# Float64 weights narrowed by a scaled upper word, and the mix as eight tiles side by side

## The chip, the core and the metric

The kernel runs on one core of a Trainium2 chip. A core has TensorE (PE, matrix products into PSUM), VectorE (DVE), ScalarE (ACT), GpSimd (POOL, which does not reach PSUM in this kernel) and SyncE (SP, whose queue issues every DMA of this kernel). Each engine has a queue of its own, filled in the order in which the program is written; semaphores hold an instruction until what it reads is written and what it overwrites is free. The metric is the device time of one execution in microseconds, as the median of several runs.

## What is computed

The inputs are q, k, v (8 batches, 8 heads, 576 rows, 64 columns), phi (the same with 32 columns), and three weight arrays. The reference, cut to what matters:

```python
a = exp(phi - phi.max(axis=2)); a /= a.sum(axis=2) + 1e-9       # softmax over the 576 rows
k_m, v_m = einsum('bhsm,bhsd->bhmd', a, k), einsum('bhsm,bhsd->bhmd', a, v)
s = q @ k_m.T / sqrt(64);  p = softmax(s, axis=-1)                # over the 32 memory slots
x = (p @ v_m) as (batch, 576, 8*64)
gate = sigmoid(sum over k<5 of conv_w[k] * x shifted down by 4-k rows)
out = (gate * (x @ w_val)) @ w_out
```

The weights w_val, conv_w and w_out come to the chip as float64 and are narrowed there to float32. Each float64 is two 32-bit words, and only integer and float32 operations are used on them.

## The kernel before

All 8 heads of a batch are handled in G = 2 groups of HG = 4 heads; four heads of 32 slots fill 128 partitions. The 576 rows are cut into two halves s of HALF = 288 columns, and the 512 channels into NP = 4 tiles t of two heads each (PG = 2 tiles for a group). The program is a set of small step functions, and the string ORDER lists every call (step, batch, group, half, tile); the engines' queues get their instructions in just that order. Where a step may run on two engines, `pick` takes the first unless the call ends in a star. So phi_sub.0.0* runs on DVE, and soft_mul.0.0 without a star on POOL.

One batch b goes as follows. The step phi_max, phi_turn, phi_top, phi_spread, phi_lay, phi_sub and phi_exp make the exponentials of phi. For each group, slots (L404) multiplies them with k, v and a column of ones; slots_inv and slots_scale divide; slots_turn (L434) transposes, slots_place copies the result; scores (L450) multiplies by q into two PSUM banks `cv`; scores_turn (L459, DVE) transposes to `st`. Then comes the softmax over the slots, for both groups in one instruction each (for batch 0 a group at a time): soft_max, soft_sub (L481), soft_exp (ACT), soft_sum, soft_inv, soft_mul (L505), and soft_turn (L510), which transposes back to `pT`. soft_high and soft_low split pT in a rounded part pH (ACT) and a rest pL (POOL). val_rows (L534) multiplies the memory values with w_val; val_high and val_low split the result into vwH and vwL; val_again appends a copy of the first 64 columns behind the last ones, so that a pair of heads can also be read rotated by one head.

The gate needs a causal convolution with 5 taps, and it is made in two ways. conv (L578) does it on PE: the taps are multiplied into the memory values (step taps, L563), and 5 x 8 products of 32 slots by 64 columns are accumulated. Its product for head j and half s goes to tile and partition half t, x = divmod((j - s) % 4, 2): in the second half the heads are rotated by one, so that the eight products (4 heads, 2 halves) lie in eight different places of the array (row group j, column half x). sigmoid (L622) follows on ACT. The second way is for group 1 of the batches in VECTOR_CONV (1 to 6): mix (L598) multiplies pT by the memory values alone, eight products of 292 columns, with t, x = divmod(j, 2) in both halves, so that the two halves of one head lie in the same place of the array. Then tap (L605) does the convolution: tap 0 on ACT (L608), taps 1 to 4 on DVE (L612), each as one instruction over both halves (128 partitions, 2 x 288 columns), with the tap's weight per partition from cwP; open_gate (L617) is the sigmoid.

The rotation of the second half is carried on: `swapped(b, g)` tells for which groups it holds, value (L633) then reads vwH and vwL 64 columns further, and project (L663) uses a second copy of w_out with its rows rotated (woH[1], woL[1]; step wo_pair, six DMAs within SBUF per pair of tiles). value is 6 products of 288 columns into a PSUM bank `b`, gated multiplies it with the gate (L642, DVE), gated_high and gated_low split it (ACT, POOL), project is 12 products, place copies to SBUF, store writes out.

The PSUM rings are the two-bank tile `cv` with 2 buffers (used by warm, scores, conv and mix) and the bank `b` with 4 (all other products). The loads wait for a free buffer in the ring `raw` (4 buffers), and the narrowing writes to the rings hH and hL (4 each).

Narrowing one weight tile (conv_w is tile c.0, of 8 x 320; w_val v.0 to v.3 and w_out o.0 to o.3, 128 x 512 each) is six instructions: narrow_bits (DVE, L269) shifts the upper word left by 3 and masks it; narrow_sign (DVE, L276) puts the upper bits back in; narrow_round (ACT, L284) scales the lower word down to a rounding count; narrow_add (POOL, L290) adds it; narrow_size (ACT, L294) squares the upper word as a float; narrow_done (DVE, L301) compares it with a threshold and multiplies. From cw_sb (the narrowed conv_w) spread_taps (L307) and turn_taps (L317) lay the taps out by PE. The step warm(n) multiplies the identity by itself n times on PE and keeps nothing; fp32 products show as two records each in the trace.

## Time and profile before

| what | us |
|---|---|
| median of 3 runs (275.67 to 277.62) | 275.68 |
| the profiled execution, its own time | 277.1 |
| its span, first to last instruction | 275.3 |
| PE busy in it | 263.3 |
| DVE busy in it | 197.2 |
| ACT busy in it | 157.9 |
| POOL busy in it | 128.1 |

The span is the time on the profile's own scale; the execution's own time lies 1.8 us above it, and 1.4 us above the median of the runs without a profile. A busy PE is not PE at its peak, since the ends of matmuls are modelled; how densely it works is read from the starts of its matmuls and from the chain of work that ended last.

### The profile page before, as it was taken

The page shows a single profiled execution, that of the slowest core. Times are in us where ns is not written, and L with a number is a line of the kernel's source. Part 1 is how long each engine was busy: PE and PEld are TensorE (multiplying, and loading weights), DVE is VectorE, ACT ScalarE, POOL GpSimd, SP SyncE. Part 2 cuts the span into 40 slices and gives each one's busy share as a digit, 9 for nine tenths or more (in the row PEclk, how much of TensorE's full clock was granted, in tenths as well). Part 3 has the DMA queues.
Part 4 walks back from the last instruction along what each step waited for, and adds up shares of the span by engine and source line. Part 5 has one row for each costly group of instructions (what it writes and reads, how often), then busy time and mean ns, then how long its engine had stood idle before and what let it go on. Part 6 is the DMA issues. An engine that isn't in the chain of part 4 may idle for free.

```text
span 275.3 us, 7706 instructions
## 1 busy us (share of the span) xinstructions
PE 263.3 (96%) x3312; PEld 227.5 (83%) x3312; DVE 197.2 (72%) x294; ACT 157.9 (57%) x265; POOL 128.1 (47%) x112
## 2 busy tenths in 40 slices
PE   7999779999899999999999999999999999999995
PEld 7879567777987988888968988898869888888995
DVE  3889999897847886697939785899589756931300
ACT  3544659766656465475666556836648655472511
POOL 4461759973425372383148152925247814252410
PEclk9979979999999999999999999999999999999999
DMA  6999972499985475065815393347632120121012
GB/s 198 369 359 416 344 254 62 146 251 258 401 318 181 172 243 207 14 255 174 297 53 192 121 355 122 114 201 236 240 127 90 45 88 2 44 88 43 2 68 107
DMA packets 13234, 49.95 MB, mean 181 GB/s; under 512 B 1672, under 2 KB 2184, under 8 KB 10256
## 3 DMA queue, kind: packets, MB, share of 16 engines
q1 hardware_dynamic: 13200, 49.46, 51.5%
q8 instruction: 26, 0.43, 0.7%
q14 instruction: 8, 0.07, 0.1%
HBM read 37.92 MB, written 9.44 MB: 172 GB/s over the span
## 4 chain that ended last, share of the span: by engine, by line
PE 79%; DVE 11%; ACT 3%; DMA 3%; issue 2%; SPq 2%; POOL 0%; POOLq 0%
PE b L663 31%; PE b L633 19%; PE cv L578 8%; PE b L404 6%; PE cv L221 5%; PE cv L450 3%; DMA woH<-woH 3%; DVE st L481 2%; PE b L534 2%; PE cv L598 2%; PE b L434 2%; DVE st L459 2%; DVE st L505 2%; DVE mm L474 2%; DVE pT L510 1%
## 5 line engine op out<-in xcount | busy, mean ns | idle before, releaser
L214 POOL TENSOR_TENSOR hL<-h,hH 128x576 fp32r<-128x576 f32 x32 | 47.6, 1495 | 76.6 <-ACT hH L211 68.8
L663 PE MATMUL b<-hL,woH 128*128 128x288 f32 x256 | 76.9, 300 | 1.9 <-DVE vwL L214 1.0
L663 PE MATMUL b<-hH,woL 128*128 128x288 f32 x256 | 75.5, 295 | 0.0
L663 PE MATMUL b<-hH,woH 128*128 128x288 f32 x256 | 75.4, 294 | 0.0
L663 PEld LDWEIGHTS b<-hL,woH 128*128 128x128 f32 x256 | 48.0, 187 | 8.4 <-issue 3.0
L642 DVE TENSOR_TENSOR h<-b,gate 128x288 f32<-128x288 f32 x64 | 27.9, 452 | 35.5 <-PE b L633 27.8
L663 PEld LDWEIGHTS b<-hH,woH 128*128 128x128 f32 x256 | 48.2, 188 | 0.0
L663 PEld LDWEIGHTS b<-hH,woL 128*128 128x128 f32 x256 | 48.1, 188 | 0.0
L211 ACT COPY o<-b 128x288 f32<-128x288 f32 x56 | 21.4, 399 | 36.7 <-PE b L663 30.8
L612 DVE SCALAR_TENSOR_TENSOR gate<-cv,cwP,gate 128x576 f32<-128x576 f32 x48 | 37.6, 814 | 4.7 <-ACT gate L608 3.9
L211 ACT CAST hH<-h 128x576 fp32r<-128x576 f32 x32 | 21.3, 673 | 22.9 <-DVE h L642 22.2
L214 POOL TENSOR_TENSOR pL<-pT,pH 128x1152 fp32r<-128x1152 f32 (+1 forms) x9 | 21.6, 2406 | 27.0 <-ACT pH L211 27.0
L633 PE MATMUL b<-pL,vwH 128*128 128x288 f32 x128 | 29.4, 311 | 0.0
L578 PE MATMUL cv<-pT,taps 32*64 32x288 f32 x800 | 27.0, 406 | 0.6 <-DVE pT L510 0.6
L633 PE MATMUL b<-pH,vwL 128*128 128x288 f32 x128 | 27.3, 294 | 0.0
L633 PE MATMUL b<-pH,vwH 128*128 128x288 f32 x128 | 27.3, 294 | 0.0
L221 PE MATMUL cv<-ident 128*128 128x128 f32 x152 | 23.0, 316 | 2.0 <-POOL ident masks.py:199 2.0
L633 PEld LDWEIGHTS b<-pL,vwH 128*128 128x128 f32 x128 | 20.1, 188 | 5.4 <-issue 2.4
L221 PEld LDWEIGHTS cv<-ident 128*128 128x128 f32 x152 | 21.7, 228 | 2.6 <-POOL ident masks.py:199 2.0
L578 PEld LDWEIGHTS cv<-pT,taps 32*64 32x64 f32 x800 | 17.4, 131 | 7.5 <-issue 2.8
L404 PE MATMUL b<-kv,e 128*32 128x129 f32 x640 | 21.5, 286 | 0.7 <-ACT e L395 0.7
L290 POOL TENSOR_TENSOR hH<-hH,hL 128x512 int32<-128x512 int32 (+1 forms) x9 | 13.1, 1461 | 17.3 <-DVE hH L276 7.2
(75 smaller groups left out, 428.5 us busy)
## 6 DMA issues: line engine op xcount, KB each, us to landing
kv<-in_kv_dram SPq DMA_DIRECT2D x16, 1032.0 KB, 8.2
out_dram<-o SPq DMA_DIRECT2D x30, 288.0 KB, 3.0
q<-in_q_dram SPq DMA_DIRECT2D x7, 1152.0 KB, 5.1
e<-in_phi_dram SPq DMA_DIRECT2D x7, 640.0 KB, 7.2
kv<-in_kv_dram SPq DMA_DIRECT2D x16, 129.0 KB, 9.1
raw<-in_w_val_dram SPq DMA_DIRECT2D x4, 512.0 KB, 6.8
raw<-in_w_out_dram SPq DMA_DIRECT2D x4, 512.0 KB, 9.2
q<-in_q_dram SPq DMA_DIRECT2D x2, 576.0 KB, 9.0
```

The lines of the kernel that those rows point to most:

```text
L211: eng.copy(out=out, in_=x) if eng is nc.scalar else eng.tensor_copy(out=out, in_=x)
L214: eng.tensor_tensor(out=out, in0=x, in1=hi.bitcast(F32), op=ALU.subtract)
L221: nc.tensor.matmul(ps[:, i % 2, 0:P], lhsT=ident, rhs=ident, start=True, stop=True)
L290: nc.gpsimd.tensor_tensor(out=a, in0=a, in1=r, op=ALU.add)
L404: nc.tensor.matmul(km[j * M:(j + 1) * M, 0:2 * D + 1], lhsT=e[:, g, j * M:(j + 1) * M, c], rhs=x[:, c, j, :], start=(c == 0), stop=(c == C ...
L434: nc.tensor.transpose(out=ps[:, x], in_=live["kvd", b, g][:, x], identity=ident)
L450: nc.tensor.matmul(sc[j * M:(j + 1) * M, s, 0:HALF], lhsT=live["kvT", b, g][rows, 0, j * M:(j + 1) * M], rhs=live["q", b][rows, g, j, :], ...
L578: nc.tensor.matmul(cv[t][x * D:(x + 1) * D, s, 0:HALF], lhsT=w[rows, i, :], rhs=p[rows, g, s * HALF + i:(s + 1) * HALF + i], start=(i == 0 ...
L612: nc.vector.scalar_tensor_tensor(out=gt, in0=x, scalar=w, in1=gt, op0=ALU.mult, op1=ALU.add)
L633: nc.tensor.matmul(vp[:, 0:HALF], lhsT=a[:, t // PG, n:n + P], rhs=p[:, g, s * HALF:(s + 1) * HALF], start=(i == 0), stop=(i == len(parts) ...
L642: nc.vector.tensor_tensor(out=live["h", b, s, y][:, i], in0=live["vp", b, s, t][:, 0:HALF], in1=live["gate", b, t][:, s], op=ALU.mult)
L663: nc.tensor.matmul(ps[:, 0:HALF], lhsT=w[:, t, n * P:(n + 1) * P], rhs=a[:, t % 2], start=(i == 0), stop=(i == len(parts) - 1))
```

## The change

The change has two parts and a new ORDER. First, narrowing: ACT now scales the upper word, read as a float, by 2^-112 (narrow_size, which comes first and writes the tile), DVE shifts that left by 3 and clears the sign (narrow_bits, now from the tile), POOL adds as before, and DVE's narrow_done takes the sign from the raw word with one AND and one OR. narrow_sign is gone; an ACT instruction now stands ahead of the first DVE one, and the raw tile is read to the end. Second, mix uses the same rotation as conv, so that its eight products lie in eight places. With that all groups of all batches are rotated: swapped is gone, val_again copies both groups in every batch, and the two halves of a mix tile hold different heads, so tap is one instruction for each half with a weight column of its own (cwP has twice the columns, and turn_taps makes them by 40 products of one column instead of 10 of two).

```diff
+    def narrow_size(w, t):
+        raw = live["raw", w, t]
+        live["na", w, t] = narrow_tile("hH", raw)
+        nc.scalar.activation(out=live["na", w, t], in_=raw[:, :, 1].bitcast(F32), func=AF.Copy, scale=2.0 ** -112)
...
     def narrow_bits(w, t):
-        raw = live["raw", w, t]
-        a = live["na", w, t] = narrow_tile("hH", raw)
-        nc.vector.tensor_scalar(out=a.bitcast(I32), in0=raw[:, :, 1], scalar1=3, scalar2=0x3FFFFFF8,
-                                op0=ALU.logical_shift_left, op1=ALU.bitwise_and)
-    @step
-    def narrow_sign(w, t):
         a = live["na", w, t].bitcast(I32)
-        nc.vector.scalar_tensor_tensor(out=a, in0=live["raw", w, t][:, :, 1], scalar=-0x40000000, in1=a,
-                                       op0=ALU.bitwise_and, op1=ALU.bitwise_or)
+        nc.vector.tensor_scalar(out=a, in0=a, scalar1=3, scalar2=0x7FFFFFFF, op0=ALU.logical_shift_left,
+                                op1=ALU.bitwise_and)
...
-    def narrow_size(w, t):
-        nc.scalar.activation(out=live["nr", w, t], in_=live["raw", w, t][:, :, 1].bitcast(F32), func=AF.Square)
...
     def narrow_done(w, t):
-        nc.vector.scalar_tensor_tensor(out=o, in0=r, scalar=TINY_HI ** 2, in1=a, op0=ALU.is_ge, op1=ALU.mult)
+        nc.vector.scalar_tensor_tensor(out=o.bitcast(I32), in0=live["raw", w, t][:, :, 1], scalar=-0x80000000,
+                                       in1=a.bitcast(I32), op0=ALU.bitwise_and, op1=ALU.bitwise_or)
...
     def turn_taps(_):
-        for x in range(2):
-            for i in range(KT):
-                nc.tensor.matmul(ps[x * D:(x + 1) * D, i], lhsT=cw_sb[:, 0, i * D:(i + 1) * D],
-                                 rhs=ident[0:H, H - HG + x:H:2], start=True, stop=True)
+        for j in range(HG):
+            for s in range(2):
+                t, x = divmod((j - s) % HG, 2)
+                for i in range(KT):
+                    nc.tensor.matmul(ps[x * D:(x + 1) * D, i, s, t:t + 1], lhsT=cw_sb[:, 0, i * D:(i + 1) * D],
+                                     rhs=ident[0:H, H - HG + j:H - HG + j + 1], start=True, stop=True)
...
     def val_again(b, g, n):
-        gs = slice(0, G if swapped(b, G - 1) else G - 1)
+        gs = slice(0, G)
...
     def mix(b):
-                t, x = divmod(j, 2)
+                t, x = divmod((j - s) % HG, 2)
...
     def tap(b, t, i):
+        for s in range(2):
+            x, w = live["cv", b, t][:, s, i:i + HALF], cwP[:, i, s, t - (NP - PG):t - (NP - PG) + 1]
+            if i == 0:
+                nc.scalar.activation(out=gt[:, s], in_=x, func=AF.Identity, scale=w)
+            else:
+                nc.vector.scalar_tensor_tensor(out=gt[:, s], in0=x, scalar=w, in1=gt[:, s], op0=ALU.mult,
+                                               op1=ALU.add)
...
     def value(b, s, t):
-            n = t % PG * P + (s * D if swapped(b, t // PG) else 0)
+            n = t % PG * P + s * D
...
     def project(b, s, n):
-        parts = [(w[s if swapped(b, t // PG) else 0], live[a, b, s, t // 2], t) for t in range(NP)
+        parts = [(w[s], live[a, b, s, t // 2], t) for t in range(NP)
```

ORDER is written anew as a whole; of its lines one shows the manner (before, then now): `scores.0.1 soft_high.0.0 val_rows.0 scores_turn.0.1 wo_high.0 soft_low.0.0 soft_max.0.1 load_w.o.3 conv.0.0` and `slots_scale.0.1* taps.0.1 slots_turn.0.1 load_kv.1.0 slots_place.0.1 phi_max.1 wo_high.1 scores.0.1 soft_mul.0.0`. Three places matter for what follows.

PE's queue from its start, before (L221 is warm, L361 and L377 turn and spread the maxima of phi, L307 and L317 are the taps, L404 is slots):

```order
L221 MATMUL cv<-ident 128x128 x7
L361 MATMUL b<-ident,mx 128x128
L221 MATMUL cv<-ident 128x128 x5
L377 MATMUL b<-ident,top 128x128
L221 MATMUL cv<-ident 128x128 x12
L307 MATMUL b<-cw_sb,pick_head 128x320 x2
L317 MATMUL b<-ident,cw_sb 64x2 x10
L221 MATMUL cv<-ident 128x128 x7
L404 MATMUL b<-kv_76,e 32x129 x20
```

and now (the same steps stand in lines 214, 352, 368, 296, 308 and 395):

```order
L214 MATMUL cv<-ident 128x128 x8
L352 MATMUL b<-ident,mx 128x128
L368 MATMUL b<-ident,top 128x128
L214 MATMUL cv<-ident 128x128 x8
L296 MATMUL b<-cw_sb,pick_head 128x320
L308 MATMUL b<-ident,cw_sb 64x1 x40
L296 MATMUL b<-cw_sb,pick_head 128x320
L214 MATMUL cv<-ident 128x128 x4
L395 MATMUL b<-kv_76,e 32x129 x20
```

The warming products between turning and spreading the maxima are gone, turn_taps has 40 products where it had 10, and one of the two spread_taps now follows it.

PE's queue ahead of the first value (L633 before, L626 now), before:

```order
L450 MATMUL cv<-q,kvT 32x288 x8
L534 MATMUL b<-w_val_sb,kvT 32x512 x8
L578 MATMUL cv<-pT_72,taps 64x288 x40
L361 MATMUL b<-ident,mx 128x128 x2
L377 MATMUL b<-ident,top 128x128 x2
L221 MATMUL cv<-ident 128x128 x11
L578 MATMUL cv<-pT_72,taps 64x288 x40
L404 MATMUL b<-kv_76,e 32x129 x20
L633 MATMUL b<-pL,vwH 128x288 x2
```

and now (L425 is slots_turn, L441 scores, L525 val_rows, L569 conv):

```order
L368 MATMUL b<-ident,top 128x128 x2
L214 MATMUL cv<-ident 128x128 x6
L569 MATMUL cv<-pT_72,taps 64x288 x40
L395 MATMUL b<-kv_76,e 32x129 x20
L395 MATMUL b<-kv_78,e 32x129 x20
L425 MATMUL b<-ident,kvd 128x128 x4
L441 MATMUL cv<-q,kvT 32x288 x8
L525 MATMUL b<-w_val_sb,kvT 32x512 x8
L569 MATMUL cv<-pT_72,taps 64x288 x40
L626 MATMUL b<-pL,vwH 128x288 x2
```

Now the second conv of batch 0 stands behind batch 1's slots of both groups, its transposes, its first scores and its val_rows, and the first value stands right behind that conv; before, the first value stood behind one slots of batch 1 alone.

DVE's queue at its start, before (the numbers tell the tiles apart; hH is the tile being narrowed, raw the loaded words, L350 is phi_max, L390 phi_sub):

```order
L269 TENSOR_SCALAR hH_112<-raw_102 8x320
L276 SCALAR_TENSOR_TENSOR hH_112<-raw_102,hH_112 8x320
L368 TENSOR_REDUCE top_125<-b_114 128x1
L269 TENSOR_SCALAR hH_130<-raw_104 128x512
L390 TENSOR_TENSOR e_100<-e_100,b_132 128x640
L269 TENSOR_SCALAR hH_153<-raw_108 128x512
L276 SCALAR_TENSOR_TENSOR hH_153<-raw_108,hH_153 128x512
L301 SCALAR_TENSOR_TENSOR cw_sb_81<-hL_110,hH_112 8x320
L269 TENSOR_SCALAR hH_159<-raw_123 128x512
L276 SCALAR_TENSOR_TENSOR hH_159<-raw_123,hH_159 128x512
L276 SCALAR_TENSOR_TENSOR hH_130<-raw_104,hH_130 128x512
```

and now (L268 is narrow_bits, L289 narrow_done, L359 phi_top, L381 phi_sub):

```order
L268 TENSOR_SCALAR hH_111<-hH_111 8x320
L359 TENSOR_REDUCE top_120<-b_118 128x1
L381 TENSOR_TENSOR e_103<-e_103,b_125 128x640
L268 TENSOR_SCALAR hH_123<-hH_123 128x512
L289 SCALAR_TENSOR_TENSOR cw_sb_81<-raw_101,hH_111 8x320
L268 TENSOR_SCALAR hH_146<-hH_146 128x512
L289 SCALAR_TENSOR_TENSOR w_val_sb_80<-raw_105,hH_123 128x512
L268 TENSOR_SCALAR hH_197<-hH_197 128x512
L289 SCALAR_TENSOR_TENSOR w_val_sb_80<-raw_109,hH_146 128x512
L289 SCALAR_TENSOR_TENSOR w_val_sb_80<-raw_115,hH_197 128x512
```

Each tile has two DVE instructions where it had three, and narrow_bits reads the tile that ACT has written instead of the raw words. Elsewhere in the order the first soft_mul of batch 0 (soft_mul.0.0) has moved from DVE to POOL; load_w.o.0 and load_w.o.1 are issued ahead of load_kv.0.1 instead of behind it; the 8 place calls that DVE did go to ACT; and every batch's softmax and mix stand at new distances.

## Rows read from the trace of the kernel before

**Rows 1.** The page of the profile: the span, and the busy time of each engine (share of the span, instructions).
```profile
span 275.3 us, 7706 instructions
...
PE 263.3 (96%) x3312; PEld 227.5 (83%) x3312; DVE 197.2 (72%) x294; ACT 157.9 (57%) x265; POOL 128.1 (47%) x112
```

**Rows 2.** Busy time in us of PE, PE's weight loads, VectorE, ScalarE and GpSimd in stretches of 10 us (in brackets the instructions), then PE's granted clock, the share of DMA time and GB/s.
```profile
10.00:20.00 10.00, 9.63 (x102) 7.96 (x100) 9.39 (x11) 4.72 (x11) 7.23 (x5) 0.83 1.03 357
20.00:30.00 10.00, 9.28 (x140) 7.65 (x140) 9.01 (x17) 5.69 (x11) 2.71 (x3) 1.00 1.02 406
30.00:40.00 10.00, 7.43 (x120) 6.07 (x105) 9.79 (x12) 6.53 (x11) 7.28 (x6) 0.87 0.93 311
...
60.00:70.00 10.00, 8.43 (x129) 6.98 (x128) 7.98 (x14) 6.97 (x12) 3.93 (x6) 1.00 1.03 287
```

**Rows 3.** The chain of work that ended last, in order of time: start, length in us, engine, tile, line, and how many records.
```profile
5.60 1.72 PE cv L221 x10
...
7.43 2.68 PE cv L221 x24
10.12 1.27 PE b L307 x4
11.38 1.04 PE b L317 x20
...
14.63 2.31 PE b L404 x40
16.95 2.47 PE cv L221 x20
...
45.83 2.58 PE b L633 x18
48.41 1.26 PE b L404 x40
...
50.66 0.22 PE b L434 x2
...
51.66 0.65 PE cv L450 x16
...
61.95 7.43 DMA woH<-woH
...
77.77 2.62 PE cv L578 x80
...
86.93 1.02 PE b L534 x16
...
97.69 1.15 PE cv L598 x16
...
259.39 12.81 PE b L663 x96
272.22 0.40 ACT o L211
```

**Rows 4.** Groups of instructions by line and shape: how many, busy us and mean ns of one, the engine's idle time before them and what ended it.
```profile
L612 DVE SCALAR_TENSOR_TENSOR gate<-cv,cwP,gate 128x576 f32<-128x576 f32 x48 | 37.6, 814 | 4.7 <-ACT gate L608 3.9
...
L642 DVE TENSOR_TENSOR h<-b,gate 128x288 f32<-128x288 f32 x64 | 27.9, 452 | 35.5 <-PE b L633 27.8 <-ACT gate L622 5.2 <-ACT gate L617 1.3
...
L390 POOL TENSOR_TENSOR e<-e,mxa 128x1280 f32<-128x1280 f32 x7 | 17.2, 2457 | 3.0 <-ACT mxa L211 3.0
...
L214 DVE TENSOR_TENSOR vwL<-b,vwH 128x512 fp32r<-128x512 f32 x16 | 10.5, 676 | 1.5 <-ACT vwH L211 1.5
...
L276 DVE SCALAR_TENSOR_TENSOR hH<-raw,hH 128x512 int32<-128x512 int32 x8 | 7.5, 947 | 0.2
L598 PE MATMUL cv<-pT,taps 32*64 32x292 f32 x96 | 7.3, 417 | 0.0
```

**Rows 5.** VectorE's instructions in order of time in the first 42 us: start, length, line, operation, shapes.
```profile
7.47 0.82 DVE L390 TENSOR_TENSOR e<-e,b 128x640 f32<-128x640 f32 x1 [0.83 <-PE b L377]
...
21.27 0.78 DVE L459 STREAM_TRANSPOSE st<-cv 128x576 f32<-128x576 f32 x1
...
22.91 0.76 DVE L481 TENSOR_TENSOR st<-st,mm 128x576 f32<-128x576 f32 x1
...
25.54 0.70 DVE L276 SCALAR_TENSOR_TENSOR hH<-raw,hH 128x512 int32<-128x512 int32 x1
...
26.90 1.39 DVE L505 TENSOR_TENSOR st<-st,ss 128x576 f32<-128x576 f32 x1
...
29.03 0.65 DVE L301 SCALAR_TENSOR_TENSOR hH<-hL,hH 128x512 f32<-128x512 f32 x1
...
31.42 1.74 DVE L481 TENSOR_TENSOR st<-st,mm 128x576 f32<-128x576 f32 x1
...
37.49 2.85 DVE L505 TENSOR_TENSOR st<-st,ss 128x576 f32<-128x576 f32 x1
40.37 0.78 DVE L510 STREAM_TRANSPOSE pT<-st 128x576 f32<-128x576 f32 x1
```

**Rows 6.** The same view around the taps of batch 2: eight instructions in a row.
```profile
99.65 6.40 DVE L612 SCALAR_TENSOR_TENSOR gate<-cv,cwP,gate 128x576 f32<-128x576 f32 x8 [0.65 <-ACT gate L608]
```

**Rows 7.** The same view, from the transposes of batch 3's scores to the transpose that ends its softmax.
```profile
115.15 1.45 DVE L459 STREAM_TRANSPOSE st<-cv 128x576 f32<-128x576 f32 x2 [0.26 <-PE cv L450]
...
125.85 1.38 DVE L510 STREAM_TRANSPOSE pT<-st 128x1152 f32<-128x1152 f32 x1
```

More of the change, by code (lines that the diff above doesn't have):

```diff
@@ L1 @@
 import math
-import struct
 from contextlib import ExitStack
@@ new lines @@
+load_phi.1 soft_sum.0.0 slots.0.1 warm.4 wo_high.0 soft_inv.0.0 wo_low.0 load_w.o.2 slots_inv.0.1 narrow_done.o.1
+slots_scale.0.1* taps.0.1 slots_turn.0.1 load_kv.1.0 slots_place.0.1 phi_max.1 wo_high.1 scores.0.1 soft_mul.0.0
+val_rows.0 narrow_size.o.2 scores_turn.0.1 phi_turn.1 warm.3 wo_low.1 val_high.0.1 phi_top.1 soft_max.0.1 val_high.0.0
+phi_spread.1 warm.6 load_kv.1.1 val_again.0.1.vwH phi_lay.1 narrow_bits.o.2 val_again.0.0.vwH narrow_round.o.2
+phi_sub.1 soft_turn.0.0 val_low.0.0 conv.0.0 soft_high.0.0 soft_sub.0.1* val_low.0.1 soft_exp.0.1 load_q.1
@@ new lines @@
+value.1.1.0 gated_low.1.0.0 load_q.3 scores_turn.2.1 phi_exp.3 value.1.1.1 soft_max.2 gated_low.1.1.1 project.1.0.0
+soft_sub.2* keep_v.2 project.1.0.2 load_phi.4 place.1.0.0 gated.1.1.0 soft_exp.2 gated.1.1.1 project.1.0.1 place.1.0.2
+soft_sum.2 gated_high.1.1.0 gated_low.1.1.0 slots.3.0 place.1.0.1 soft_inv.2 store.1.0.0 val_rows.2 load_kv.4.0
+slots_inv.3.0 soft_mul.2* slots_scale.3.0* project.1.1.3 val_high.2.0 taps.3.0 val_high.2.1 soft_turn.2
+val_again.2.0.vwH val_again.2.1.vwH project.1.1.2 val_low.2.0 soft_high.2 mix.2 val_low.2.1 val_again.2.0.vwL
@@ new lines @@
+phi_exp.4 val_again.3.0.vwL project.2.1.2 soft_inv.3 place.2.0.0 place.2.0.3 soft_mul.3* store.2.0.1 slots.4.1
+place.2.1.2 soft_turn.3 slots.4.0 slots_inv.4.1 soft_high.3 mix.3 load_kv.5.0 phi_max.5 project.2.0.1 tap.3.2.0
+soft_low.3 slots_inv.4.0 slots_scale.4.1* tap.3.2.1 slots_scale.4.0* phi_turn.5 project.2.1.0 place.2.0.1 tap.3.2.2
+tap.3.3.0 load_kv.5.1 taps.4.0 tap.3.2.3 value.3.0.2 place.2.1.0 tap.3.2.4 project.2.1.3 phi_top.5 open_gate.3.2
+tap.3.3.1 slots_turn.4.1 project.2.1.1 store.2.0.0 tap.3.3.2 place.2.1.3 gated.3.0.2 slots_place.4.1 store.2.1.1
@@ new lines @@
+tap.3.3.3 slots_turn.4.0 place.2.1.1 value.3.0.3 slots_place.4.0 store.2.1.0 tap.3.3.4 scores.4.0 val_rows.4
+open_gate.3.3 scores_turn.4.0 phi_spread.5 gated.3.0.3 val_high.4.0 conv.3.0 phi_lay.5 val_low.4.0 val_again.4.0.vwH
+val_high.4.1 phi_sub.5 gated_high.3.0.1 val_low.4.1 value.3.1.2 sigmoid.3.0 value.3.1.3 sigmoid.3.1 gated.3.1.2
+gated_low.3.0.1 phi_exp.5 scores.4.1 gated.3.1.3 value.3.0.0 scores_turn.4.1 load_q.5 val_again.4.1.vwH
+val_again.4.1.vwL value.3.0.1 val_again.4.0.vwL soft_max.4 keep_v.4 value.3.1.0 gated_high.3.1.1 gated.3.0.0 slots.5.1
@@ L185 @@
     cwB = const.tile([P, G, KT * D], F32, name="cwB")
-    cwP = const.tile([P, KT, PG], F32, name="cwP")
+    cwP = const.tile([P, KT, 2, PG], F32, name="cwP")
     pick_head = const.tile([H, H, M], F32, name="pick_head")
@@ L195 @@
     steps = {}
-    def swapped(b, g):
-        return g != G - 1 or b not in VECTOR_CONV
     def step(fn):
```

206 lines of the change are left out of this document (89 added, 117 removed).

## Prediction

> **What bounds the kernel now.** I read the page first: PE is busy 96% of the span, DVE 72%, the others less [rows 1]. An average hides stages, so next the busy times in stretches of 10 us: from 10 to 40 us DVE is busy 9.0 to 9.8 of 10 [rows 2]. PE is also busy there, but mostly with warming products, which nobody needs. The chain of work that ended last gives the border: the first value starts at 45.83 us, and from there the chain is almost all PE until its last record ends at 259.39 + 12.81 = 272.20; 3.1 us for the last copy and store close the span at 275.3 [rows 1, 3]. So the kernel has two stages: a start of 45.8 us set by the chain through DVE, and 272.2 - 45.8 = 226.4 us set by PE. PE's only sizeable idle time in the second is in 60 to 70 us, where it is busy 8.4 of 10 and waits for the copies of w_out within SBUF [rows 2, 3]. Each edit is therefore judged by its stage.
>
> **The mix.** It is 1.15 us for 16 records, the same kind of product as conv, which has 2.62 us for 80 [rows 3]. A fifth of conv is 0.524 us; with 292 columns for 288, 0.53. The difference is in the places: conv uses eight, mix four, twice. The mix takes conv's places, so I price it by conv: 1.15 - 0.53 = 0.62 us less, six times, 3.7 us, all in the stage that PE sets. The bounds are nothing and 3.7.
>
> A rule of the Trainium skill speaks against it. TensorEngine Tiling (Array Packing), section Restrictions and Gotchas, states that different row tiles cannot access the same PSUM bank simultaneously. In both kernels two row groups write each bank (tile t, half s), so by that rule the eight products would still take two turns, and the sum would lose its 3.7 us. conv's row speaks for the other side, since its products share banks in the same manner.
>
> **The taps on DVE.** 48 instructions of 814 ns become 96 of half the size [rows 4]. No row shows that form at 288 columns. A half costs at least 407 ns, if nothing in the 814 is fixed, and at most 814. The nearest row is the gating product, also 288 columns from PSUM, at 452 ns [rows 4]. I take 0.45 us: 96 x 0.45 - 48 x 0.81 = 4.3 us more on DVE in all, 0.7 us a batch. It hides as long as conv of the same batch need not wait: conv needs both cv tiles, which the last tap frees. In the new order PE has between mix.1 and conv.1.0 four projects, three values and small transposes, 9.2 us (4 x 1.6, 3 x 0.8, 0.4, at the eight projects in the last 12.8 us of rows 3 and three values in 2.58), 10.0 and 10.4 in batches 2 and 3. Sixteen halves are 7.2 us, and the two first taps on ACT about 1: 8.2, hidden by a margin of 1.0. Before, eight took 6.40 [rows 6].
>
> **Other work that grows or shrinks beside PE.** val_again copies both groups (POOL is busy 47%), eight place copies go from DVE to ACT (57%); both hide in these engines' idle time [rows 1], and I cost them at nothing. If a late copy on POOL held a value, it would be under 1 us each. Narrowing sheds nine narrow_sign (eight of 947 ns [rows 4] and a small one, 8 us of DVE); the later narrow_done has the same form as narrow_sign. All of that lies in the first stage.
>
> **The start.** turn_taps grows from 20 to 80 records. At the 1.04 us that 20 took, 80 take 4.2 us, 3.1 more [rows 3]. What hides it are warming products that go: between the two transposes of the maxima stood 1.72 us of them, and 24 records of 2.68 follow [rows 3], where now there are 16 in all. By these rows the first slots start at 14.7 against 14.63. PE's granted clock is 0.83 in 10 to 20 us and 0.87 in 30 to 40 [rows 2]; eighty tiny products may hold it down, which the 2.31 us of the first slots already contain, against 1.26 for the same work later [rows 3].
>
> From there I compare DVE's lists between two points: the transposing of the first scores (21.27, [rows 5]) and the one that frees the second conv. Before, that one is soft_turn.0.1, ending at 40.37 + 0.78 = 41.15: 19.9 us, nearly dense. Now it is the transposing of scores.1.0, one instruction behind soft_turn.0.1, since scores.1.0 holds a cv buffer that this conv needs. The list in between loses two narrow_sign (1.4) and one soft_mul (1.39, now on POOL), has four narrow_done at 0.70 for one of 0.65 (+2.15), and gains two val_low (1.35), one transpose (0.78) and four short instructions of the division (0.6) [rows 4, 5]: +2.1 us, 22.0 in all. The first point comes about 1 us earlier, at 20.3, because seven warming products instead of ten stand between slots and scores (ten took 2.47, [rows 3]). So the second conv starts at 42.3 + 0.2 and the first value behind it at 42.5 + 2.6 = 45.1.
>
> Two things move that. Two-input operations last longer beside POOL: 1.74 against 0.76 for the same soft_sub, 2.85 against 1.39 for soft_mul [rows 5]. Without such overlap the new list is some 2.3 us shorter, and the first value at 42.8. On the other side, the new order hangs batch 1's slots, division, transposes and scores in front of that conv, a chain through ACT, PE and DVE that waits for POOL's subtraction of 2.46 us [rows 4], and POOL now also has soft_mul.0.0. w_out's first two tiles are loaded ahead of the second group's k and v, whose DMA must wait at SP until narrow_done has released raw tiles: 1 MB at 406 GB/s is 2.6 us [rows 2], landing just ahead of its use. I put 0.7 us on it and take **45.8 us, the same as before**; the bounds are 42.8 and 49.
>
> **The sum.** At its first value PE has by then done more than before: one slots (1.26), two slots_turn (0.44), one scores (0.65), one val_rows (1.02), 3.4 us that no longer stand behind it [rows 3]. So PE's second stage is 226.4 - 3.4 - 3.7 = 219.3 us. The wait for w_out's copies ended about 2 us late before; now the softmax of batch 1 should be late by about as much at mix.1, so no term. The softmax of batch 3 takes from 115.15 to 127.23, 12.1 us [rows 7], while the new order has only 10.8 us of PE work between its scores and its mix (12.4 before): 1.0 us. Together 45.8 + 219.3 + 1.0 + 3.1 = 269.2 against the span of 275.3: 6.1 us less. The profiled execution's own time is 277.1, 1.4 above the median of 275.68; I take the difference off the median: **269.6 us**.
>
> **The rivals.**
>
> *The mix gains nothing.* By a mechanism that serves products of one bank in turn, mix stays at 1.15 us: 269.6 + 3.7 = 273.3 us. Against it: conv at 33 ns a record beside mix at 72 (2.62 over 80, 1.15 over 16, [rows 3]). Chance 0.04. That is the Trainium skill's rule on banks (TensorEngine Tiling, section Restrictions and Gotchas) as a result; by the conv row, the trace disagrees.
>
> *The start eats it.* If batch 1's chain in front of the second conv brings the first value only at 51 us or later, the gain is gone: 269.6 + 5.2 = 274.8 us. For it: DVE is dense there, and one late POOL or DMA step moves everything behind. Against it: 51 needs 5 us beyond a list of DVE that is only 2.1 us longer. Chance 0.14.
>
> *The split taps set the pace; slower.* If a half costs 0.7 us instead of 0.45, taps last 16 x 0.7 + 1 = 12.2 us, and conv waits 3.0, 2.2 and 1.8 us in batches 1 to 3, and some 2 in 5 and 6 each; the values that wait for gates hold their banks besides, so some 10 us: 279.6. The point from which it decides: above 0.51 us a half the margin of batch 1 is gone, and at about 0.65 the whole gain. For it: 814 ns is the upper bound; against it: 452 ns for the nearest shape [rows 4]. Chance 0.08.
>
> **How the numbers follow.** My forecast, with smaller starts and stalls around it, has 0.74. The first value at 42.8 and no stall gives 265.6; at 48.8 with 3 us of stalls 274.6; the first two rivals lie inside. **Range 265.6 to 274.6.** About 1% is what a measurement of this kernel can tell from no change, 2.8 us. Faster by more than that needs under 272.9: 0.74. Within 1%: the late start, the mix without gain, 0.17. Slower: 0.09, the taps and a little for what I don't see.
>
> **What would show it.** Mix at 0.53 us for 16 records, or 1.15. First value near 45.8 us. Taps: mean near 450 ns, and no wait of conv for cv in the batches' middle. From the first value to PE's last record some 220 us. No stall over 1.5 us at mix.3. The prediction fails if the first value is past 50 us, if PE waits at each conv, or if PE's idle time grows at the mixes because the softmax now stands too close to them.

## The result, and the profile after

The changed kernel takes 278.64 us (median of 20 runs, 276.48 to 282.26) against 276.94 for the kernel before (20 runs beside them): ratio 1.0058, 95% interval 1.0036 to 1.0081. The forecast was 269.6, in a range from 265.6 to 274.6. The profiled execution of after is one of its quickest, 276.93 us with a span of 275.2; its granted clock was 0.994 on average, in most of the other runs 0.974 to 0.988, so its profile does not show all of the loss. Ratios compare the runs of a kernel that lie near its fastest; of less_warm below, three of seven runs, the profiled one among them, took 278.0 to 279.2 us at a granted clock of 0.969, the other four 271.7 to 272.7 at 0.987.

The page of after, which answers to [rows 1]: span, and busy time of each engine.

```profile
span 275.2 us, 7826 instructions
...
PE 260.8 (95%) x3338; PEld 224.4 (82%) x3338; DVE 187.1 (68%) x324; ACT 158.1 (57%) x275; POOL 130.9 (48%) x121
```

VectorE has 10 us less to do, and the span is the same. The chain of work that ended last, kernel after: start, length in us, engine, tile, line, records. It answers to [rows 3]; L359 is phi_top, L296 spread_taps, L308 turn_taps, L214 warm, L395 slots, L569 conv, L626 value, L604 the taps on DVE, L589 mix, L656 project.

```profile
6.07 0.30 DVE top L359
...
9.01 0.73 PE b L296 x2
9.74 3.93 PE b L308 x80
...
14.40 2.00 PE cv L214 x8
16.41 1.94 PE b L395 x40
...
38.34 1.77 PE b L395 x54
40.11 0.57 issue
...
44.80 2.23 PE cv L569 x64
47.03 3.02 issue
50.04 0.74 PE cv L569 x16
...
64.42 6.70 DMA e<-in_phi_dram
...
72.55 6.13 DVE gate L604 x15
...
98.52 0.68 PE cv L589 x16
...
259.29 12.81 PE b L656 x96
```

The first value starts at 50.04 + 0.74 = 50.8 us (45.83 before), and PE's last record ends at 272.1 as it did before. So PE's second stage is 221.3 us for 226.4, 5.1 less, and the start has taken back 5.0. Two pieces of it stand in the chain: turn_taps and the warming products behind it, which bring the first slots to 16.41 (14.63 before); and a stop of 3.02 us inside the second conv, behind "issue", where PE waits for nothing that the profile shows (one of 0.57 us stands in the slots before). Further on, the taps of batch 1 begin only at 72.55, since phi_max.3 stands ahead of them on DVE and waits for its load.

Groups by line and shape, after, which answer to [rows 4]: count, busy us and mean ns, idle time before.

```profile
L604 DVE SCALAR_TENSOR_TENSOR gate<-cv,cwP,gate 128x288 f32<-128x288 f32 x96 | 41.7, 508 | 2.1 <-ACT gate L602 2.0
L589 PE MATMUL cv<-pT,taps 32*64 32x292 f32 x96 | 4.5, 430 | 0.0
L308 PE MATMUL b<-ident,cw_sb 8*64 8x1 f32 x80 | 4.0, 193 | 0.0
```

Half a tap takes 508 ns, not 450. The mix's 16 records take 0.68 us (chain), not 0.53 and not 1.15.

### The profile page after: what moved, and what is told of

Read it like the earlier page. It is cut to its first block, busy times and chain, and to the rows that moved or that the text cites. A ratio compares the mean times of both kernels' runs of the same rounds, so it can differ in the third digit from the quotient of the medians.

```text
span 275.2 us, 7826 instructions
## 1 busy us (share of the span) xinstructions
PE 260.8 (95%) x3338; PEld 224.4 (82%) x3338; DVE 187.1 (68%) x324; ACT 158.1 (57%) x275; POOL 130.9 (48%) x121
## 4 chain that ended last, share of the span: by engine, by line
PE 76%; DVE 14%; issue 3%; ACT 3%; DMA 2%; POOL 0%; ACTq 0%; POOLq 0%; DVEq 0%
PE b L656 30%; PE b L626 17%; PE cv L569 9%; PE b L395 6%; PE cv L441 3%; DVE st L472 3%; PE cv L214 3%; DMA e<-in_phi_dram 2%; DVE gate L604 2%; PE b L525 2%; PE b L308 1%; PE b L425 1%; DVE ss L483 1%; DVE mm L465 1%; PE cv L589 1%
## 5 line engine op out<-in xcount | busy, mean ns | idle before, releaser
L207 POOL TENSOR_TENSOR hL<-h,hH 128x576 fp32r<-128x576 f32 x32 | 48.4, 1521 | 66.0 <-ACT hH L204 56.4
L656 PE MATMUL b<-hL,woH 128*128 128x288 f32 x256 | 77.5, 303 | 1.1 <-DVE h L635 0.6
L656 PE MATMUL b<-hH,woL 128*128 128x288 f32 x256 | 75.5, 295 | 0.0
L656 PE MATMUL b<-hH,woH 128*128 128x288 f32 x256 | 75.3, 294 | 0.0
L635 DVE TENSOR_TENSOR h<-b,gate 128x288 f32<-128x288 f32 x64 | 27.3, 450 | 43.0 <-PE b L626 32.6
L656 PEld LDWEIGHTS b<-hL,woH 128*128 128x128 f32 x256 | 48.0, 187 | 8.5 <-issue 4.1
L204 ACT COPY o<-b 128x288 f32<-128x288 f32 x64 | 25.0, 399 | 40.5 <-PE b L656 33.5
L656 PEld LDWEIGHTS b<-hH,woH 128*128 128x128 f32 x256 | 48.2, 188 | 0.0
L656 PEld LDWEIGHTS b<-hH,woL 128*128 128x128 f32 x256 | 48.1, 188 | 0.0
L604 DVE SCALAR_TENSOR_TENSOR gate<-cv,cwP,gate 128x288 f32<-128x288 f32 x96 | 41.7, 508 | 2.1 <-ACT gate L602 2.0
L569 PE MATMUL cv<-pT,taps 32*64 32x288 f32 x800 | 27.9, 406 | 3.6 <-issue 3.0
L204 ACT CAST hH<-h 128x576 fp32r<-128x576 f32 x32 | 21.4, 673 | 14.9 <-DVE h L635 14.2
L626 PE MATMUL b<-pL,vwH 128*128 128x288 f32 x128 | 29.4, 311 | 0.0
L626 PE MATMUL b<-pH,vwL 128*128 128x288 f32 x128 | 27.3, 294 | 0.0
L626 PE MATMUL b<-pH,vwH 128*128 128x288 f32 x128 | 27.3, 294 | 0.0
L569 PEld LDWEIGHTS cv<-pT,taps 32*64 32x64 f32 x800 | 17.5, 131 | 11.3 <-issue 5.1
L626 PEld LDWEIGHTS b<-pL,vwH 128*128 128x128 f32 x128 | 20.1, 188 | 6.0 <-issue 3.8
L395 PE MATMUL b<-kv,e 128*32 128x129 f32 x640 | 21.5, 283 | 1.9 <-ACT e L386 1.4
L395 PEld LDWEIGHTS b<-kv,e 128*32 128x32 f32 x640 | 18.2, 139 | 5.1 <-issue 2.3
L381 POOL TENSOR_TENSOR e<-e,mxa 128x1280 f32<-128x1280 f32 x7 | 18.3, 2618 | 6.1 <-ACT mxa L204 6.0
L626 PEld LDWEIGHTS b<-pH,vwL 128*128 128x128 f32 x128 | 20.5, 188 | 0.0
```

The lines of the kernel that those rows point to most:

```text
L204: eng.copy(out=out, in_=x) if eng is nc.scalar else eng.tensor_copy(out=out, in_=x)
L207: eng.tensor_tensor(out=out, in0=x, in1=hi.bitcast(F32), op=ALU.subtract)
L381: eng.tensor_tensor(out=t, in0=t, in1=mxa.unsqueeze(3).to_broadcast(list(t.shape)), op=ALU.subtract)
L395: nc.tensor.matmul(km[j * M:(j + 1) * M, 0:2 * D + 1], lhsT=e[:, g, j * M:(j + 1) * M, c], rhs=x[:, c, j, :], start=(c == 0), stop=(c == C ...
L569: nc.tensor.matmul(cv[t][x * D:(x + 1) * D, s, 0:HALF], lhsT=w[rows, i, :], rhs=p[rows, g, s * HALF + i:(s + 1) * HALF + i], start=(i == 0 ...
L604: nc.vector.scalar_tensor_tensor(out=gt[:, s], in0=x, scalar=w, in1=gt[:, s], op0=ALU.mult, op1=ALU.add)
```

## The experiments

Fifteen more kernels were measured, each beside the kernel before. The table has for each the ratio to before, and from the chain of its profiled execution the start of the first value, the end of PE's last record and the stage between them. The kernels whose second stage is that of before show 226.4 to 227.1 for it, those with that of after 220.5 to 221.4, which tells how far two profiles of the same agree: differences under 0.9 us are not told apart.

| kernel | ratio (95%) | records of turn_taps | first value | last record ends | second stage |
|---|---|---|---|---|---|
| before | 1 | 20 | 45.8 | 272.2 | 226.4 |
| after | 1.006 (1.004, 1.008) | 80 | 50.8 | 272.1 | 221.3 |
| turn_long | 1.018 (1.014, 1.022) | 80 | 51.3 | 277.8 | 226.6 |
| mix_only | 1.017 (1.013, 1.020) | 80 | 51.8 | 277.4 | 225.6 |
| mix_25 | 1.002 (0.9995, 1.005) | 50 | 46.9 | 272.4 | 225.5 |
| taps_25 | 0.978 (0.974, 0.983) | 50 | 44.1 | 265.5 | 221.4 |
| taps_15 | 0.973 (0.969, 0.978) | 30 | 45.6 | 266.6 | 221.0 |
| turn_late | 0.983 (0.979, 0.988) | 80 (later) | 45.8 | 266.3 | 220.5 |
| late_15 | 0.977 (0.972, 0.982) | 30 (later) | 43.8 | 265.1 | 221.3 |
| order_oldmix | 0.983 (0.979, 0.988) | 20 | 44.1 | 266.8 | 222.7 |
| taps_joined | 0.975 (0.970, 0.979) | 30 | 45.5 | 265.8 | 220.2 |
| old_narrow | 0.999 (0.996, 1.002) | 30 | 52.3 | 273.1 | 220.8 |
| narrow_only | 1.010 (1.006, 1.013) | 20 | 48.0 | 274.5 | 226.5 |
| narrow_top | 1.013 (1.008, 1.018) | 20 | 49.0 | 276.0 | 227.1 |
| narrow_ahead | 1.003 (0.9999, 1.006) | 20 | 46.0 | 272.6 | 226.6 |
| kv_late | 1.018 (1.016, 1.021) | 80 | 49.1 | 277.1 | 228.0 |
| less_warm | 0.983 (0.979, 0.988) | 80 | | | |

The table has no times of less_warm; its profile is read below only for where its stop falls.

### turn_taps: shorter, longer, elsewhere

taps_25 makes the same table of taps by 25 products instead of 40:

```diff
-        for j in range(HG):
-            for s in range(2):
-                t, x = divmod((j - s) % HG, 2)
+            for x, s, t, n, j in ((0, 0, 0, 2, 0), (1, 0, 0, 2, 1), (0, 1, 0, 2, 1), (1, 1, 0, 1, 2), (1, 1, 1, 1, 0)):
...
```

> The changed kernel with turn_taps in 25 products instead of 40 (pairs of heads in one product where their order allows it; the result is the same). 30 records fewer at 49 ns are 1.5 us: the first slots start at 14.9 instead of 16.3 and, if that chain sets the start, the first value comes 1 to 1.5 us earlier; PE's instructions move by 60, so a late fetch should hit another place, and still cost some 2 to 3 us. Ratio to the kernel before 0.997 to 1.004. Rival, that turn_taps is hidden: first value unchanged.

Between the medians lie 8.4 us (278.64 and 270.27), between the last records of the two profiles 6.6, all of them in the start: the second stage is the same. That is far more than 30 records less give by their own length (1.5 us at 49 ns each), so turn_taps was tried by itself. turn_long is the kernel before with

```diff
-        for x in range(2):
+        for x in [0, 1] * 4:
```

> The kernel before, in which turn_taps alone is longer: each of its ten products is issued four times into the same place, 80 records for 20, as many as the change has. Nothing else differs. If the length of turn_taps stands on the path (theory one), it takes 4 to 6.4 us where it took 1.04, the first slots start 4 to 6.5 us later, and the first value and the end with it: 281 to 283.5 us, ratio 1.015 to 1.023. By the prediction's step (warming products hide it, and the start is set by VectorE's list): the warming products behind it are not fewer here, so at most 3.1 us more, and ratio 1.000 to 1.011.

The kernel before loses 4.5 us, from the lengthened turn_taps alone: 5.59 us for 1.04. The warming products behind it hide nothing, since they too must run before the first slots. taps_15 shortens turn_taps further, with products of four, three and one columns:

```diff
+            for x, m, n, j in ((0, 0, 4, 0), (1, 0, 3, 1), (1, 3, 1, 0)):
+                nc.tensor.matmul(ps[x * D:(x + 1) * D, i, m:m + n], ..., rhs=ident[0:H, k:k + n], ...)
```

> The changed kernel with turn_taps in 15 products of four, three or one column (30 records), everything else as in the change. Compared with the 25-product version (50 records, 1.84 us, ratio 0.978): 20 records at 37 to 52 ns are 0.7 to 1.0 us. Theory one: the first slots start 0.7 to 1 us earlier, ratio 0.972 to 0.979. If the start is by then set by another chain (VectorE's list, the loads), or if the fetch of PE's instructions holds the first values until the same time, nothing more comes: 0.976 to 0.982.

Here the first slots came later than with 25 (14.44 for 12.91): the granted clock was at its lower level from 11.2 to 18.0 us, for 13.0 to 16.5. The times are not told apart (0.973 and 0.978, with intervals that overlap). turn_late keeps the 40 products and moves them behind the first scores:

```diff
-... spread_taps.0 ... turn_taps.0 place_taps.0 ... lay_taps.0 slots.0.0 ...
-... phi_spread.0.1 warm.16 ... phi_exp.0.1 ...
+... phi_spread.0.1 turn_taps.0 ... phi_exp.0.1 lay_taps.0 ...
```

> The changed kernel with its 40-product turn_taps, moved: it stands where sixteen warming products stood (22.4 to 26.1 us in the changed kernel) instead of ahead of the first slots, and lay_taps behind the second phi_exp. Its result is first read by the taps of batch 1. Theory one (the change loses because the 80 records stand ahead of the first slots, and lower the clock there): the first slots start at 12 to 13 us for 16.4, as with the 25 products or earlier, and the time is that of the 15-product version within 1%: ratio 0.967 to 0.982. Rival (what counts is the number of products or the narrowing of the weights, wherever the products stand): 0.995 to 1.006.

The chain of work that ended last, turn_late, up to 25 us:

```profile
3.05 9.83 DMA kv<-in_kv_dram
...
13.01 1.94 PE b L395 x40
...
20.02 3.94 PE b L308 x80
...
23.98 0.17 ACT cwP L204
24.16 0.59 ACT hH L263
```

The same 80 records, 3.94 us as before, no longer stand ahead of the first slots, which start at 13.0, released by the load of k and v; the first value comes at 45.8. So most of the price was the place ahead of the first slots. It is not all of it: the records are in the chain again, since lay_taps on ACT (L204) waits 2.2 us for them, narrow_size (L263) stands behind it, and DVE's narrow_bits waits 1.5 us for that. The first value is 1.7 us later than in taps_25, whose slots start at the same time. late_15 does both.

> The changed kernel with turn_taps in 15 products and moved to the place of the sixteen warming products, as in turn_late. If moving and shortening add up: ratio 0.966 to 0.972. If one of them already takes turn_taps off the path, and the low clock behind missing warming products costs about as much: 0.972 to 0.985.

The first value, 43.8, is the earliest of all, but the ratio, 0.977, is not told apart from either alone. The loads are next in line: the second slots wait 2.1 us for k and v, whose load ends at 22.29 in the chain.

The length of the train also hangs on PE's clock. Busy times in stretches of 2 us (PE, weight loads, DVE, ACT, POOL), then the granted clock, DMA share and GB/s. In mix_only:

```profile
10.00:12.00 2.00, 1.91 (x19) 1.30 (x19) 1.97 (x4) 1.41 (x4) 1.50 (x1) 1.00 1.02 276
12.00:14.00 2.00, 2.00 (x30) 2.00 (x28) 2.00 (x3) 0.46 (x1) 1.80 (x2) 0.56 0.99 317
14.00:16.00 2.00, 2.00 (x24) 2.00 (x25) 0.32 (x1) 0.00 (x0) 1.44 (x1) 0.50 1.08 428
...
20.00:22.00 2.00, 2.00 (x25) 1.70 (x28) 0.34 (x1) 0.00 (x0) 1.27 (x1) 0.50 1.01 351
```

and in the kernel after:

```profile
12.00:14.00 2.00, 2.00 (x38) 1.88 (x37) 0.85 (x2) 0.17 (x1) 1.64 (x1) 1.00 1.02 361
14.00:16.00 2.00, 2.00 (x10) 1.67 (x8) 0.38 (x1) 0.99 (x2) 0.00 (x0) 0.58 1.03 399
```

In mix_only the clock falls to its lower level (1.2 of 2.4 GHz) soon after turn_taps has begun, and stays there to 22 us: the 80 records last 6.34 us, 79 ns each. In after it falls only when they are done: 49 ns each, and the eight warming records behind them last 251 ns each. Either way the price is in front of the first slots.

### The stop in the second conv

> The changed kernel with its 40-product turn_taps, but with one warming product instead of sixteen behind the first scores (22.4 to 26.1 us in the changed kernel): 60 fewer instructions ahead of PE's instruction number 1217, at which PE stood still for 3.0 us in the second conv. Nobody waits for these products. Theory two (PE ran out of instructions, because the DMA that brings the next 256 waited some 7 us behind the data loads and came at 47.5 us): PE reaches number 1217 sixty instructions later in the program, among the first values; that fetch still lands near 48.6 us, the stop shortens to some 1 us, the first value starts at 47 to 48.5 us and the time is 2 to 3 us under the changed kernel's: 275.5 to 277 us, ratio 0.994 to 1.001. Rival (the stop belongs to conv.0.1 itself, its taps or its buffer): the stop stays at 3 us in the same conv, ratio 1.003 to 1.009. A lower clock behind the missing products could cost 1 us in either case.

```diff
-... phi_spread.0.1 warm.16 ...
+... phi_spread.0.1 warm.1 ...
```

The chain of work that ended last, less_warm:

```profile
49.83 2.76 PE cv L569 x80
52.58 2.05 PE b L626 x14
54.63 1.17 issue
```

and taps_25, which has 60 of PE's instructions less ahead of that conv too:

```profile
41.33 2.76 PE cv L568 x80
44.08 2.05 PE b L625 x14
46.13 0.65 issue
```

In both the conv runs in 2.76 us, and a shorter stop falls among the values. Counting all of PE's instructions in the trace (matmuls, weight loads and 67 others), it comes behind number 1217 in after, less_warm and taps_25 alike; with 60 taken out ahead of it, it fell 60 later in the program. So it belongs to a place in the instruction stream and not to conv, its taps or its buffer. What is special there shows in the DMA queues. PE's instructions come by a queue of their own (q8), 26 packets of 16 KB for 6,743 instructions. The view of DMA queues of the kernel after, first for 39.2 to 47.4 us, then for 47.4 to 50.1 (queue, packets, MB, share):

```profile
q1 hardware_dynamic: 373, 2.29, 86.4%
```

```profile
q1 hardware_dynamic: 298, 0.63, 98.3%
q8 instruction: 1, 0.02, 2.6%
```

While the loads had the DMA engines 86% busy, no packet of instructions came for 8 us; the next landed at 48.59 us, and PE went on at 50.04, 1.45 later. The 0.57 us at 40.11 fall behind number 961, 256 ahead. In taps_25 the stop ends 1.48 us behind its packet's landing (45.30), and a stop of 1.32 us behind number 961 in kv_late, below, 1.48 us behind the packet at 40.78. Before, the DMA's share was low (32% in 40 to 50 us, 4% in 43.9 to 46), and the packet came 0.4 us after PE had reached number 961, in time; it came 7.6 us after it in the kernel after. The Trainium skill (Runtime: NRT & Kernel Launch, section Instruction fetch mechanics) states that instructions are refilled in blocks of 16 KiB and that the cost of a boundary is mostly hidden. The packets' size agrees; that the cost is hidden does not hold here, where it was 3.0 us.

That the loads delay the packet was tried from their side too: kv_late issues load_kv.2.0 and load_kv.2.1 behind load_q.2.

```diff
-... load_kv.2.0 ... load_kv.2.1 ... load_q.2 ...
+... load_q.2 load_kv.2.0 load_kv.2.1 ...
```

> The changed kernel with the loads of k and v for batch 2 held back behind the load of q for batch 2, so that the DMA engines are idle for some us before the first value. Theory of late instruction fetch: the packet of PE's own instruction queue that came at 47.5 us comes some 5 us earlier, the wait of 3.0 us inside the second conv falls under 0.5, the first value comes at 47 to 48 us instead of 50.7; what follows at the copies of w_out and the load of phi may take back a part; ratio to the kernel before 0.993 to 1.003, about 2 to 3 us under the changed kernel. Rival, that PE waits there for a buffer or another engine: wait and first value stay.

The stop in the conv is gone (2.71 us for all 80 records, first value 1.7 us earlier), though one of 1.32 us is left in the slots before. But k and v of batch 2 then come late, and the time misses what was expected. The chain, kv_late:

```profile
40.94 1.32 issue
...
46.38 2.71 PE cv L569 x80
49.10 4.16 PE b L626 x30
...
57.53 11.03 DMA woH<-woH
...
68.62 7.55 DMA e<-in_phi_dram
```

The later loads, of w_out's copies and phi, have moved into the path, and the second stage is 6.7 us longer: a wait moved, not removed. less_warm as a whole is some 6 us faster than after (0.983 and 1.006), more than was expected and more than the 2 us by which its stop is shorter; without a trace of a run of 272 us the rest stays unexplained.

### The mix and the split taps

mix_only is the kernel before, with its order, in which turn_taps, mix, tap, val_again, value and project are those of the change; mix_25 is the same with 25 products in turn_taps.

> The order of before with the new mix alone: eight places, split taps, 40 products in turn_taps, both groups copied in val_again. Mix 0.68 us for 16 records. Theory: the mixes give back 6 x 0.47 = 2.8 us, but in this order PE has only 8.0 us of work between a mix and the next conv, and two first taps on ACT with 16 halves of about 0.49 us last 8.9, so conv waits 0.5 to 1.5 us in five batches: ratio 0.998 to 1.012. Rival, that split taps cost nothing: no gap at conv, ratio 0.988 to 0.992.

> The mix, the split taps and the copies of the change in the order of the kernel before, as in mix_only, but turn_taps in 25 products of one or two columns (50 records) instead of 40 of one column. Theory one: what mix_only lost (ratio 1.0167) is turn_taps, 5.3 us, and the low clock behind it, 1.1 us; with 50 records 4.5 to 5.5 us come back and the six faster mixes show: ratio 0.992 to 0.999, first value at 46 to 47.3 us. Rival: the split taps and the extra copies cost what mix_only lost; then the ratio stays above 1.008.

The sixteen records take 0.68 us in four of the six mixes of mix_25, 0.74 and 0.79 in batches 1 and 5. mix_only's loss is turn_taps, since mix_25 is back at 1.002; but in this order the faster mix is worth at most 0.9 us of the second stage, for the 2.8 of its rows. The rest went into waits behind it: in mix_25 PE is idle 1.1 us longer in that stage than before, most of all behind mix.1, where it waits 1.3 us for the split first taps on ACT, and the convs behind the later mixes are together 0.7 us longer. In the changed order the question is asked the other way: order_oldmix has the order and narrowing of after with the mix, taps and turn_taps of before, and taps_joined is taps_15 with each tap as one instruction over both halves (the second half's own weights left out):

```diff
 order_oldmix, in mix
-                t, x = divmod((j - s) % HG, 2)
+                t, x = divmod(j, 2)
 taps_joined, in tap
-        for s in range(2):
-            x, w = live["cv", b, t][:, s, i:i + HALF], cwP[:, i, s, t - (NP - PG):t - (NP - PG) + 1]
+        x, w = live["cv", b, t][:, :, i:i + HALF], cwP[:, i, 0, t - (NP - PG):t - (NP - PG) + 1]
```

> The changed kernel's order and narrowing with the mix, taps, turn_taps (ten products) and copies of before. Against the 15-product version (ratio 0.9734) it lacks the rotated mix and the split taps and has ten products less. If the mix is worth what its own rows say, 6 x 0.47 = 2.8 us, less 0.4 us for the shorter turn_taps: ratio 0.979 to 0.984. If the mix gains nothing on the path: 0.970 to 0.975. If the whole gain over before is the mix and not the order: 0.990 or above.

> The 15-product version with each tap as one instruction over both halves again (48 of 576 columns for 96 of 288), with the weights of the first half for both; what it leaves out is the second half's own weights. If the split taps (508 ns a half, above the 0.51 us from which the prediction had them decide) hold conv back, 1.5 to 4 us are gained: ratio 0.960 to 0.968. If VectorE's 4 us lie beside PE, as the prediction took them, nothing: 0.969 to 0.978.

The chains, order_oldmix and then taps_joined, around batch 1's mix (x16) and the conv behind it (x80):

```profile
61.53 1.15 PE cv L590 x16
...
72.08 2.98 PE cv L570 x80
```

```profile
62.94 0.68 PE cv L588 x16
...
73.02 3.28 PE cv L568 x80
```

The new order without the new mix has a second stage of 222.7 us, 3.7 less than before; the rotated mix brings it to 221.0 (taps_15), 1.7 more, of the 6 x 0.47 = 2.8 that its rows promise; the ratios, 0.983 and 0.973, are told apart. With joined taps it is 220.2. Of these 0.8 us 0.5 show in the trace, where conv.1.0 waits for the last tap: with its waits it lasts 3.85 us in taps_15 and 3.35 in taps_joined, for 2.68 in the later batches. The rest is within what two profiles differ by, and the measured ratios of taps_joined and taps_15 are not told apart.

### The narrowing

narrow_only is the kernel before with the new narrowing, in the order of before; narrow_size stands ahead of each narrow_bits.

```diff
-narrow_bits.o.2 phi_turn.1 narrow_sign.o.2 narrow_bits.o.3 narrow_add.o.2 phi_top.1
+narrow_size.o.2 narrow_bits.o.2 phi_turn.1 narrow_size.o.3 narrow_bits.o.3 narrow_add.o.2 phi_top.1
```

> The order of before with the new narrowing alone (ACT scales the upper word where the first DVE instruction stood, narrow_sign is gone). DVE sheds some 7 us of work in the first 46 us. If the start is set by DVE's work, the first value comes 2 to 4 us earlier than 45.8 and the ratio to before is 0.985 to 0.993. If the start is set by chains that hand over between engines and by loads, the first value stays within 1 us of 45.8 and the ratio is 0.997 to 1.003.

```profile
34.07 1.28 ACT L621
...
35.36 0.65 ACT gate L621
36.01 1.12 ACT hH L269 x2
...
37.15 1.49 DVE hH L274
38.65 0.34 DVE top L367
...
39.03 0.69 PE b L376 x2
39.72 4.32 PE cv L220 x22
```

In this chain of narrow_only, narrow_size (L269) stands behind two sigmoids on ACT (L621), DVE's narrow_bits (L274) waits for it, phi_top (L367) stands behind that, and PE waits for phi_top. Behind it eleven warming products (L220), at a granted clock of 0.50, stand ahead of the second conv for 4.32 us more. narrow_top moves narrow_bits of o.2 and o.3 behind phi_top.1 on DVE; narrow_ahead instead moves narrow_size ahead of the sigmoid on ACT:

```diff
 narrow_top
-... narrow_bits.o.2 phi_turn.1 narrow_size.o.3 narrow_bits.o.3 narrow_add.o.2 phi_top.1
+... phi_turn.1 narrow_size.o.3 phi_top.1 narrow_bits.o.2 narrow_bits.o.3 narrow_add.o.2
 narrow_ahead
-... sigmoid.0.1 narrow_size.o.2 narrow_bits.o.2 phi_turn.1 narrow_size.o.3 ...
+... narrow_size.o.2 narrow_size.o.3 sigmoid.0.1 narrow_bits.o.2 phi_turn.1 ...
```

> The new narrowing in the order of before, as in narrow_only, but VectorE's phi_top.1 stands ahead of narrow_bits of the tiles o.2 and o.3. In narrow_only these two waited 2.4 us for ScalarE, which had a sigmoid to do first, and PE waited behind phi_top.1, 4.8 us for 1.7. Theory: this queueing is the whole loss of narrow_only (ratio 1.0096); 3 us come back, first value near 45 us: ratio 0.994 to 1.001. Rival (the new narrowing is slower in itself, on ScalarE or by its DMA release): stays above 1.005.

> As narrow_only (the new narrowing in the order of before), but narrow_size of the tiles o.2 and o.3 stands ahead of the first sigmoid on ScalarE instead of behind it. If the wait of VectorE for ScalarE (2.4 us behind that sigmoid in narrow_only, moved to the next instructions in narrow_top) is the whole loss, the first value comes at 44 to 46 us for 48.0, and the ratio is 0.990 to 1.001. If the new narrowing is slower in itself, it stays at 1.005 to 1.013.

narrow_top missed: PE no longer waits at phi_top, but DVE does at narrow_bits as before, only with the softmax behind it, and the first value is at 49.0. narrow_ahead takes the wait away where it arises, and 2.1 us of 2.2 come back in the first value. The loss of narrow_only is that queueing; in the order of before the new narrowing is then worth nothing measurable. In the changed order it is worth much: old_narrow is taps_15 with the six instructions of before, narrow_sign behind each narrow_bits and the squaring between narrow_add and narrow_done:

```diff
-narrow_size.X ... narrow_bits.X ... narrow_add.X ... narrow_done.X
+narrow_bits.X narrow_sign.X ... narrow_add.X ... narrow_size.X ... narrow_done.X
```

> The 15-product version of the changed kernel (ratio 0.973) with the narrowing of before put into its order: narrow_sign behind each narrow_bits, the squaring on ScalarE half way between narrow_add and narrow_done. If the new narrowing relieves VectorE at the start, nine instructions of 0.65 to 0.95 us come back into a list that is dense there: first value 3 to 7 us later, ratio 0.985 to 0.998. If VectorE's list does not set the start, 0.970 to 0.978.

The chain, old_narrow, where it differs most (L274 is narrow_sign, L577 conv, L634 value):

```profile
36.07 2.93 DVE hH L274
...
39.84 4.17 PE cv L577 x80
...
52.25 4.16 PE b L634 x30
```

The first value is 6.6 us later than in taps_15 and the second stage the same. The narrow_sign of 2.93 us runs beside POOL's subtraction (36.00 to 38.45); the median of its kind is 0.69. The granted clock falls to 0.50 in the conv behind it, which lasts 4.17 us where taps_15 has 2.69. The order shown is mine for this narrowing; a better one may exist.

## Why the prediction was wrong

**The step that failed** is the one on the start: "What hides it are warming products that go [...] By these rows the first slots start at 14.7", and with it the first value at 45.8. Measured are 16.41 and 50.8. The growth of turn_taps was sized well (4.2 us forecast, 3.93 measured); what was to make up for it was not. Of the warming products that go between the turning of the maxima and spread_taps the forecast took back some 2.6 us, and 1.55 came back (from 6.04 to 9.01 us for 5.60 to 10.12), since PE now waits there for phi_top. The eight warming records behind turn_taps took 2.00 us at the lower clock, for 2.21 of fourteen before. Nor had the range a bound for turn_taps: its 4.2 us were a price at full clock, and at the lower level it lasted 5.6 and 6.3 (turn_long, mix_only).

The larger part is a term that stood in no step: PE's stops for its instructions. Of the 5.0 us, 0.9 lie ahead of the transposing of the first scores (21.20, forecast 20.3), 0.7 from there to the second conv, with the stop of 0.57, and 3.4 in that conv, with the stop of 3.02.

Both hang on the long train. With the 80 records elsewhere (turn_late) or fewer (taps_25, taps_15) the first value is at 44.1 to 45.8. Comparing after with taps_25, the first slots are 3.5 us later (16.41 for 12.91) and the stop in conv adds 3.2, 6.7 in all. Why most of the stop goes with the shorter train is not shown: the DMA is as busy in taps_25, but the packet came 4.7 us after number 961 was reached, for 7.6.

Between forecast and median lie 9.0 us. The start has 5.0 of them and the second stage 1.0. The other 3.1 are the step from a profiled execution to a median: 1.4 us were taken off, as before, but the profiled execution of after lies 1.7 below its median, and no trace shows what its slower runs lose.

**VectorE's list** came out as worked: from the transposing of the first scores to the second conv 22.9 us were forecast, with the 0.7 for batch 1's chain, and 22.8 measured in taps_25 and taps_15, 23.6 in after with the stop of 0.57 in it. Inside it, the terms on narrowing were too small: the list was said to lose 1.4 us by narrow_sign and gain 2.15 by narrow_done, where the old narrowing costs 6.6 us in the same order. A two-input instruction beside POOL (2.93 us for 0.69), the lower clock in the conv behind it and what else it held up were not in that count.

**The second stage** was forecast at 226.4 - 3.4 - 3.7 + 1.0 = 220.3 and is 221.3. Work done earlier: 3.4 forecast, 3.7 measured for the order as a whole (order_oldmix). The mix: the eight places do run side by side, but 0.68 us is not a fifth of conv's 2.62, so 2.8 us by its rows instead of 3.7, and 1.7 of them in the stage. The rival that the mix gains nothing is out: with two row groups on each bank as before, the records took 0.68 us where they had taken 1.15. The Trainium skill, TensorEngine Tiling (Array Packing), section Restrictions and Gotchas, states that different row tiles cannot access the same PSUM bank simultaneously. The trace disagrees with the 1.15 us that the prediction had by it. Whether the bank has a part in the way from 0.53 to 0.68 was not tried. The taps at 508 ns are just at the 0.51 from which they were to decide, and cost some 0.5 us, at conv.1.0 alone; the rival that they set the pace is out. The stall of 1.0 us at mix.3 did not come.

**The rival "the start eats it"** has the right place and nearly the right point (51 us), by another mechanism: not batch 1's chain on DVE, but the train of tiny products and the late packets of PE's instructions. That its 51 us is near 50.8 is luck. Its 274.8 us lay just outside the range that was said to hold it.

## What to carry to other kernels

Before an added train of products is called hidden by work that goes, ask what is queued behind it, and whether the engine waited for something in the place of what goes. Work whose result is needed 60 us later belongs where the engine waits, and so does what takes the result away: in turn_late a small copy on ACT held up the narrowing. A change that is good in its parts (order with narrowing 3.7 us and mix 1.7 in the second stage, narrowing 6.6 in the start of that order) can be undone by one cheap helper in the start: taps_15, the same change with 15 products for 40, takes 269.36 us, 0.973 of before. And where an engine stops behind nothing, compare the DMA queue of its instructions with the loads.
